# More attention units by rows, a fourth buffer for P, and group loads in the queue of the turns

## The chip, the cores and the metric

The kernel runs on one core of one Trainium2 chip. Its time is the device time of one execution in microseconds (us); medians over several executions are given, with lowest and highest. All runs here are of the state "fast" (on one core there is no second die to compare with). A change counts as faster or slower from 2% on; the effects in this case are far smaller, so ratios are given with a 95% interval.

## The reference

One transformer block for 2048 tokens of width 512, in bfloat16: a grouped-query attention with cached K and V (32 query heads, 8 K/V heads of 128, 2048 keys), then a gated MLP. Both are wrapped in a layer norm whose shift, scale and gate rows come from a condition vector `c`.

```python
mod = (_silu(c) @ w_mod).reshape(c.shape[0], 6, 1, -1)      # sa, ca, ga, sb, cb, gb
h = _layernorm(x, axis=-1) * (1 + ca) + sa
x = x + ga * _A_ref(h, A_k_cache, A_v_cache, A_wq, A_wo)    # attention
h = _layernorm(x, axis=-1) * (1 + cb) + sb
x = x + gb * _B_ref(h, B_w_in, B_w_sp, B_b_sp, B_w_out)     # gated MLP
# in _A_ref:
scores = jnp.einsum('bhqd,bhkd->bhqk', q, k) * Dh ** (-0.5)
p = _softmax(scores, axis=-1)
o = jnp.einsum('bhqk,bhkd->bhqd', p, v)
```

`ga` and `gb` matter below: they are the two rows of the modulation that the kernel spreads over all 128 partitions, by way of the chip's main memory.

## The kernel before

The attention is a loop over **units**. A unit is 128 queries of one K/V group with its four heads; there are 128 of them (16 query tiles for each of 8 groups). A unit has eight **slots**. In each slot TensorE (PE) computes two score matmuls of this unit, ScalarE (ACT) the exponential of them, and PE then does an eighth of the PV product (probabilities times V) of an *earlier* unit and some filler (Q projection or output projection Wo).

There are two kinds of unit:

- **plain**: scores with keys on partitions. PV can use the exponentials as they are, in 64 matmuls of 129 columns, whose extra column of ones gives the softmax sums.
- **by rows**: scores with queries on partitions. ACT writes each head's row into one of six *row buffers* and sums it as it goes, VectorE (DVE) divides the row by its sum, and a transposing DMA, a **turn** of 128 x 2048, issued by SyncE (SP), puts it with keys on partitions into the unit's P buffer. PV is then 16 matmuls of 512 columns, cheaper on PE (8.64 against 8.80 us for the unit in the trace of before), but it needs all four turns to have landed.

```python
TURN_A, TURN_B = 2 * CT, NU - 2                # 8 and 126

def by_rows(u):
    return TURN_A <= u < TURN_B and u % 2 == 0

def pv_at(u):                                  # in which unit the PV of u runs
    return u + 3 if by_rows(u) else u + 1

users, homes = dict(pT0=-2, pT1=-1, wsp=CT + 2), {}   # three P buffers
for u in range(NU):
    homes[u] = min(users, key=lambda k: users[k])
    assert users[homes[u]] < u
    users[homes[u]] = pv_at(u)

def turn_rows(u, hh):                          # two slots after the head's last exponential
    # ... tot = sum of the two halves, rinv = 1 / tot (DVE)
    rows = rows_of(u, hh)
    nc.vector.tensor_scalar(out=rows, in0=rows, scalar1=rinv, scalar2=None, op0=ALU.mult)
    nc.sync.dma_start_transpose(out=pTs[u][:, :, hh * P : (hh + 1) * P], in_=rows)
```

Work that is not of the rhythm itself is put into a calendar, `at(unit, slot, function)`, which sets its place in the program. Four entries matter below. The modulation rows `ga` and `gb` are computed in unit 5, written to main memory as 512 values of 4 bytes each, and read back onto all partitions. The weights of each next group are loaded by GpSimd (POOL), behind a one-element copy that makes POOL wait for a unit's turns (up to 113.4 us in the trace). The first weight matrix of the MLP, `win_sb`, 1792 KB, is loaded in unit 126; three of the six row buffers lie in its place.

```python
def mod_rows():
    # ... mod_part(0), mod_part(1): 32 matmuls of one column
    for i, (part, rows) in enumerate(((2, ga_rows), (5, gb_rows))):
        cols = slice(part * NDT, (part + 1) * NDT)
        nc.vector.tensor_copy(out=modc[:, cols], in_=mc_ps[:, i * NDT : (i + 1) * NDT])
        line = dram.tile([D], FP32, name=f"mod{part}")
        nc.gpsimd.dma_start(out=line[:].rearrange("(dt p) -> p dt", p=P), in_=modc[:, cols])
        nc.gpsimd.dma_start(out=rows[:], in_=line[:].partition_broadcast(P))

at(NU - 2, 4, lambda: nc.gpsimd.dma_start(out=win_sb, in_=win_dram))
at(4, 4, mod_cols_b)
at(5, 4, mod_rows)
# ... for each later group: at(u + 1, 5, after_rows(u)), then at(u + 1, 5, load) on POOL
```

## Time and profile before

| | before |
|---|---|
| median of 3 runs | 1313.34 us (1312.97 to 1314.31) |
| span of the profiled execution | 1311.5 us |
| start to unit 8 | 81.73 us |
| units 8 to 13 | 49.40 us |
| units 14 to 111 | 854.56 us |
| units 112 to 126 | 129.63 us |
| from unit 127 to the end (last PVs, MLP) | 196.16 us |

Below the first two rows, a unit begins with its first exponential on ACT, taken from the trace's records; the last five rows add up to the span. (In the middle this reads 8.87 and 8.57 for the two kinds; the prediction counts from PE's first scores and has 8.64 and 8.80. The pairs are the same.)

PE carries the time almost alone, as the prediction shows with the page's lines. What it does not show is the list of DMA issues, with the median time from issue to landing as the last figure. I had not read these three lines of the kernel before as a warning:

```profile
oT<-onorm SPq DMA_TRANSPOSE x69, 2.8
...
hT<-xn SPq DMA_TRANSPOSE x12, 6.1
...
mod<-modc POOLq DMA_DIRECT2D x2, 2.0 KB, 12.7
```

Only one transfer of the kernel, a load of 1 KB (1.8 us), is smaller than the two writes of the modulation rows, and these took the longest to land. Transposes of the same size, 128 x 512, land in 2.8 us in one place and in 6.1 in another.

### The profile page before, as it was taken

What the parts mean: (1) busy time and instruction counts of PE and PEld (TensorE: products, weight loads), DVE (VectorE), ACT (ScalarE), POOL (GpSimd) and SP (SyncE); (2) the same over time, 40 slices, a digit from 0 to 9 for tenths busy, and PEclk for the clock granted to TensorE, in tenths of its full rate; (3) what the DMA queues carried; (4) which work ended last, traced back from release to release, by engine and by line L of the source; (5) the groups of instructions that cost most, each with busy time, mean ns of one, the idle gap of its engine ahead of it and who ended that gap; (6) DMA issues with size and microseconds to landing.
All of it is one profiled execution on the core that took longest, in us unless ns stands there. A gap on an engine that the chain in (4) does not pass through costs nothing.

```text
span 1311.5 us, 24369 instructions
## 1 busy us (share of the span) xinstructions
PE 1303.8 (99%) x9527; PEld 736.9 (56%) x9527; DVE 689.5 (53%) x1693; ACT 1113.0 (85%) x1533; POOL 59.4 (5%) x115
## 2 busy tenths in 40 slices
PE   9999999999999999999999999999999999999998
PEld 5665555555555555555555555555555555644445
DVE  5644455444454544444445454444445588784444
ACT  7899999999999999999999999999999999550000
POOL 1200000000000000000000000000000011120000
PEclk9999999999999999999999999999999999999999
DMA  6669778877897677867886778668876688364300
GB/s 181 154 97 157 130 128 154 158 118 133 158 166 149 121 144 155 144 125 140 160 169 122 133 157 156 125 127 153 175 143 125 118 140 144 103 133 96 82 21 27
DMA packets 607723, 174.45 MB, mean 133 GB/s; under 512 B 597264, under 2 KB 603664, under 8 KB 607600
## 3 DMA queue, kind: packets, MB, share of 16 engines
q1 hardware_dynamic: 600576, 153.67, 64.9%
q0 software_dynamic: 4432, 16.91, 4.1%
q10 hardware_dynamic: 2592, 2.23, 0.5%
q8 instruction: 77, 1.26, 0.4%
q14 instruction: 46, 0.38, 0.1%
HBM read 21.89 MB, written 2.10 MB: 18 GB/s over the span
## 4 chain that ended last, share of the span: by engine, by line
PE 96%; DVE 2%; DMA 1%; POOL 0%; issue 0%; ACT 0%; DVEq 0%; POOLq 0%
PE o_ps L1080 19%; PE s_ps L1024 18%; PE s_ps L1005 16%; PE o_ps L1059 16%; PE misc L1112 8%; PE misc L945 8%; PE misc L1456 7%; PE s_ps L1290 1%; PE o_ps L1477 1%; DVE stz L1312 1%; PE s_ps L1477 1%; DMA xnT<-xn 0%; DMA wmod_a<-in_w_mod_dram 0%; DVE z L686 0%; POOL rstd_lnz L682 0%; PE misc L855 0%
## 5 line engine op out<-in xcount | busy, mean ns | idle before, releaser
L1031 ACT ACTIVATE pT<-s_ps 128x1024 bf16<-128x1024 f32 x552 | 561.1, 1025 | 30.7 <-PE s_ps L1024 8.7
L1080 PEld LDWEIGHTS <-pT 128*128 128x128 bf16 x4416 | 295.3, 98 | 128.9
L1080 PE MATMUL o_ps<-v,pT 128*128 128x129 bf16 x4416 | 339.7, 220 | 0.0
L1024 PE MATMUL s_ps<-qT,kT 128*128 128x512 bf16 x1104 | 328.1, 379 | 0.3 <-ACT pT L1031 0.2
L1005 PE MATMUL s_ps<-kT,qT 128*128 128x512 bf16 x944 | 280.7, 379 | 0.0
L1012 ACT ACTIVATE win_sb<-s_ps 128x1024 bf16<-128x1024 f32 x238 | 243.7, 1025 | 3.5
L1112 PE MATMUL misc<-wo_g,oT 128*128 128x512 bf16 x512 | 194.0, 379 | 0.0
L945 PE MATMUL misc<-hT,wq_g 128*128 128x512 bf16 (+2 forms) x520 | 187.0, 371 | 0.1
L1024 PEld LDWEIGHTS <-kT 128*128 128x128 bf16 x1104 | 107.3, 98 | 114.9 <-issue 2.3
L1012 ACT ACTIVATE pn<-s_ps 128x1024 bf16<-128x1024 f32 x156 | 159.6, 1024 | 2.0 <-ACT wmod_a L1012 0.3
L1059 PEld LDWEIGHTS <-v 128*128 128x128 bf16 x944 | 92.4, 98 | 111.4
L956 DVE CAST qT<-misc 128x512 bf16<-128x512 f32 x125 | 85.7, 686 | 122.8 <-PE misc L945 122.8
L1068 DVE CAST oT<-o_ps 128x512 bf16<-128x512 f32 x59 | 40.8, 692 | 194.9 <-PE o_ps L1059 194.9
L1059 PE MATMUL o_ps<-wsp,v 128*128 128x512 bf16 x480 | 142.1, 379 | 0.0
L1059 PE MATMUL o_ps<-pT,v 128*128 128x512 bf16 x464 | 138.0, 379 | 0.0
L1005 PEld LDWEIGHTS <-qT 128*128 128x128 bf16 x944 | 92.2, 98 | 61.6
L1045 DVE TENSOR_TENSOR tot<-rs 128x1 f32<-128x1 f32 x236 | 36.4, 154 | 127.1 <-ACT win_sb L1012 84.8
L1456 PE MATMUL misc<-wsp,z 128*128 128x512 bf16 (+2 forms) x560 | 101.4, 336 | 0.2
L1050 DVE TENSOR_SCALAR win_sb<-win_sb,rall 128x2048 bf16<-128x2048 bf16 x119 | 89.7, 753 | 4.4 <-DVE rall L1048 0.3
L1012 ACT ACTIVATE wmod_a<-s_ps 128x1024 bf16<-128x1024 f32 x78 | 79.9, 1025 | 0.0
L1456 PEld LDWEIGHTS <-z 128*128 128x128 bf16 x560 | 50.5, 98 | 49.4 <-DVE z L686 1.6
L1125 DVE TENSOR_TENSOR xacc<-misc,xacc 128x512 f32<-128x512 f32 x112 | 76.2, 680 | 0.0
(110 smaller groups left out, 824.1 us busy)
## 6 DMA issues: line engine op xcount, KB each, us to landing
v<-in_A_v_cache_dram POOLq DMA_DIRECT2D x7, 512.0 KB, 6.6
wq_g<-in_A_wq_dram POOLq DMA_DIRECT2D x7, 512.0 KB, 3.9
wo_g<-in_A_wo_dram POOLq DMA_DIRECT2D x7, 512.0 KB, 4.5
wsp<-in_w_mod_dram POOLq DMA_DIRECT2D x1, 2048.0 KB, 9.1
out_dram<-yout ACTq DMA_DIRECT2D x16, 128.0 KB, 1.7
win_sb<-in_B_w_in_dram POOLq DMA_DIRECT2D x1, 1792.0 KB, 8.0
x_sb<-in_A_x_dram SPq DMA_DIRECT2D x3, 512.0 KB, 6.1
oT<-onorm SPq DMA_TRANSPOSE x69, 2.8
```

The source lines that it names most:

```text
L945: nc.tensor.matmul(ps[0][:, o0 : o0 + n], lhsT=wqs[g][:, dt, hh * DH : (hh + 1) * DH], rhs=hTs[ch][:, dt, c0 : c0 + n], start=(dt == 0), s ...
L956: nc.vector.tensor_copy(out=dst, in_=src)
L1005: nc.tensor.matmul(s_ps[:, c * 512 : (c + 1) * 512], lhsT=qTs[b][:, hh, jj * P : (jj + 1) * P], rhs=groups[g]["kT"][:, k0 : k0 + 512], sta ...
L1012: nc.scalar.activation(out=rows_of(u, hh)[:, half * HK : (half + 1) * HK], in_=s_ps[:], func=ACT.Exp, scale=inv_sqrt_dh, accum_out=rsums[u ...
L1024: nc.tensor.matmul(s_ps[:, h * 512 : (h + 1) * 512].rearrange("p (r q) -> p r q", r=REP), lhsT=groups[g]["kT"][:, kt * P : (kt + 1) * P], ...
L1031: nc.scalar.activation(out=pTs[u][:, 2 * i : 2 * i + 2, :], in_=s_ps[:].rearrange("p (k q) -> p k q", k=2), func=ACT.Exp, scale=inv_sqrt_dh,)
L1050: nc.vector.tensor_scalar(out=rows, in0=rows, scalar1=rinv, scalar2=None, op0=ALU.mult)
L1059: nc.tensor.matmul(o_pss[u][:], lhsT=groups[g]["v1"][:, kt, 0:DH], rhs=pTs[u][:, kt, :], start=(kt == 0), stop=(kt == NKT - 1),)
L1080: nc.tensor.matmul(o_ps[:, hh % 2, 0 : DH + 1], lhsT=pTs[u][:, kt, hh * P : (hh + 1) * P], rhs=groups[g]["v1"][:, kt, 0 : DH + 1], start=( ...
L1112: nc.tensor.matmul(X_ps[:], lhsT=oTs[u][:, hh, :], rhs=groups[g]["wo"][:, hh, :], start=(hh == 0), stop=(hh == REP - 1),)
L1125: nc.vector.tensor_tensor(out=xaccs[j][:], in0=X_ps[:], in1=xaccs[j][:], op=ALU.add)
L1456: nc.tensor.matmul(g_ps[:, :n], lhsT=z2[:, st, f * P : (f + 1) * P], rhs=wsp[t][:, st, c0 : c0 + n], start=(st == 0), stop=(st == NT - 1 a ...
```

## The change

The intent is to cut PE's work further. In units 8 to 111 three of five units go by rows instead of one of two, 69 in all instead of 59. So that turns may come closer together, *every* unit in that stretch has its PV three units later; that needs a fourth P buffer. The 2 MB of `x` are not needed between the first layer norm and the last group, so their place is taken, and `x` is loaded again in the last group. The group loads move from POOL to SP, the queue of the turns, and need no waiting copies there. The modulation moves from units 4 and 5 to unit 9, the first unit without PV work, and the load of `win_sb` a little earlier.

```diff
+    TURN_A, TURN_B = 2 * CT, (HKV - 1) * NT
+    kinds = [
+        TURN_A <= u < TURN_B and (u - TURN_A) % 5 in (0, 2, 3)
+        or TURN_B <= u < NU - CT and u % 2 == 1
+        for u in range(NU)
+    ]
     def pv_at(u):
-        return u + 3 if by_rows(u) else u + 1
+        return u + 3 if TURN_A <= u < TURN_B or by_rows(u) else u + 1
-    users, homes = dict(pT0=-2, pT1=-1, wsp=CT + 2), {}
+    users, homes = dict(pT0=-2, pT1=-1, x=TURN_A + 1, wsp=TURN_A + 2), {}
...
+        at(it, 5, rows)        # mod_b(it): the writes of ga and gb, by POOL
+        for k, (part, dst) in enumerate(((2, ga_rows), (5, gb_rows))):
+            at(it + 4 + k, 5, ... nc.sync.dma_start(...))          # the read-backs, by SP
...
-    at(NU - 2, 4, lambda: nc.gpsimd.dma_start(out=win_sb, in_=win_dram))
-    at(4, 4, mod_cols_b)
-    at(5, 4, mod_rows)
+    at(NU - 3, 6, lambda: nc.gpsimd.dma_start(out=win_sb, in_=win_dram))
+    mod_b(TURN_A + 1)
...
+        it, q = (g - 1) * NT, nc.gpsimd if g == 1 else nc.sync
+        at(*((5, 0) if g == 1 else (it + 5, 5)), lambda g=g, q=q: load_v(g, q))
         # ... load_wq at it + 7, load_wo at it + 9, in the same way
+    for ch in range(NCH):      # x again
+        at(TURN_B + 2 + 2 * ch, 5, ... nc.sync.dma_start(out=x_sb[...], in_=x_dram[...]))
```

(Not printed here: the helper signatures, the fillers' places, when Wo follows.)

More of the change, by code (lines that the diff above doesn't have):

```diff
@@ L723, in load_wq, with load_v @@
         )
-    def load_v(g):
+    def load_v(g, engine):
         v1 = late.tile([P, NKT, DV], BF16, name="v1")
@@ L728, in load_v @@
         if g > 0:
-            nc.gpsimd.dma_start(out=v1[:, :, 0:DH], in_=v_dram[:, g])
+            engine.dma_start(out=v1[:, :, 0:DH], in_=v_dram[:, g])
         else:
@@ L759 @@
     nc.sync.dma_start_transpose(out=kT0[:, HK:SK], in_=A_k_cache[0, 0, HK:SK])
-    load_v(0)
+    load_v(0, nc.sync)
     for ch in range(1, NCH):
@@ L963 @@
     NU = HKV * NT
-    TURN_A, TURN_B = 2 * CT, NU - 2
-    def by_rows(u):
-        return TURN_A <= u < TURN_B and u % 2 == 0
+    TURN_A, TURN_B = 2 * CT, (HKV - 1) * NT
[4 more added lines that the diff above has]
+    ]
+    by_rows = kinds.__getitem__
     def pv_at(u):
-        return u + 3 if by_rows(u) else u + 1
+        return u + 3 if TURN_A <= u < TURN_B or by_rows(u) else u + 1
     def wo_at(u):
-        return pv_at(u) + (3 if u < TURN_B - CT else 2)
-    users, homes = dict(pT0=-2, pT1=-1, wsp=CT + 2), {}
+        return pv_at(u) + (3 if u < NU - 2 * CT else 2)
+    users, homes = dict(pT0=-2, pT1=-1, x=TURN_A + 1, wsp=TURN_A + 2), {}
     for u in range(NU):
-        homes[u] = min(users, key=lambda k: users[k])
+        if u == TURN_B:
+            del users["x"]
+        homes[u] = min(users, key=users.get)
         assert users[homes[u]] < u
@@ L995, in qk @@
                 pTs[u] = wspp.tile([P, NT, 512], BF16, name="wsp")
+            elif homes[u] == "x":
+                pTs[u] = x_sb
             else:
@@ L1038, in rows_of @@
     def rows_of(u, hh):
-        return pn[((u - TURN_A) // 2 * REP + hh) % len(pn)][:, 0:SK]
+        return pn[(sum(kinds[:u]) * REP + hh) % len(pn)][:, 0:SK]
     def turn_rows(u, hh):
@@ L1167, in ln2, with mod_b, begin, cols @@
         at(it + 2, 5, third)
-    def mod_cols_b():
-        mc_ps = bank("misc")
-        for i in range(2):
-            mod_part(i, wmod_b, (1 + i) * D, mc_ps)
-        mod_copy(3, mc_ps)
-    def mod_rows():
-        mc_ps = bank("misc")
-        for i, row in enumerate((0, 3)):
-            mod_part(i, wmod_b, row * D, mc_ps)
-        for i, (part, rows) in enumerate(((2, ga_rows), (5, gb_rows))):
-            cols = slice(part * NDT, (part + 1) * NDT)
-            nc.vector.tensor_copy(out=modc[:, cols], in_=mc_ps[:, i * NDT : (i + 1) * NDT])
-            line = dram.tile([D], FP32, name=f"mod{part}")
-            nc.gpsimd.dma_start(out=line[:].rearrange("(dt p) -> p dt", p=P), in_=modc[:, cols])
-            nc.gpsimd.dma_start(out=rows[:], in_=line[:].partition_broadcast(P))
+    def mod_b(it):
+        ps, lines = {}, {}
+        def begin(k):
+            ps[k] = bank("misc")
+            mod_part(0, wmod_b, (D, 0)[k], ps[k])
+        def cols():
+            mod_part(1, wmod_b, 2 * D, ps[0])
+            mod_copy(3, ps[0])
+        def rows():
+            mod_part(1, wmod_b, 3 * D, ps[1])
+            for i, part in enumerate((2, 5)):
+                c = slice(part * NDT, (part + 1) * NDT)
+                nc.vector.tensor_copy(out=modc[:, c], in_=ps[1][:, i * NDT : (i + 1) * NDT])
+                lines[part] = dram.tile([D], FP32, name=f"mod{part}")
+                nc.gpsimd.dma_start(
+                    out=lines[part][:].rearrange("(dt p) -> p dt", p=P), in_=modc[:, c]
+                )
+        at(it, 1, lambda: begin(0))
+        at(it, 2, cols)
+        at(it, 4, lambda: begin(1))
+        at(it, 5, rows)
+        for k, (part, dst) in enumerate(((2, ga_rows), (5, gb_rows))):
+            at(
+                it + 4 + k,
+                5,
+                lambda part=part, dst=dst: nc.sync.dma_start(
+                    out=dst[:], in_=lines[part][:].partition_broadcast(P)
+                ),
+            )
     def load_wsp(tile_, t, st):
@@ L1229 @@
     at(2, 5, lambda: nc.gpsimd.dma_start(out=wmod_b, in_=wmod_dram[:, :, 2 * D : NMOD]))
-    at(NU - 2, 4, lambda: nc.gpsimd.dma_start(out=win_sb, in_=win_dram))
-    at(4, 4, mod_cols_b)
-    at(5, 4, mod_rows)
+    at(NU - 3, 6, lambda: nc.gpsimd.dma_start(out=win_sb, in_=win_dram))
+    mod_b(TURN_A + 1)
     def set_fill(b):
-        hole = TURN_A + 1 if (TURN_A + 1) // CT == b - 1 else None
+        hole = TURN_A + 2 if (TURN_A + 2) // CT == b - 1 else None
         fs = qproj(b, list(range(REP)), 0, 512, ("misc", "o_ps" if hole else "misc"))
@@ L1241, in set_fill @@
             if hole:
-                it, slot = divmod(hole * NSLOT + k // 2 - 1, NSLOT)
+                it, slot = hole, k // 2
             if b == 1:
@@ L1254 @@
         at(NU + 1 + st // 4, 2 * (st % 4), lambda st=st: load_wsp(wsp[0], 0, st))
-    def after_rows(u):
-        seen = stat.tile([1, 1], BF16, name="seen")
-        nc.gpsimd.tensor_copy(out=seen[:], in_=pTs[u][0:1, NKT - 1, 511:512])
     def after_pv(u):
@@ L1265 @@
     for g in range(1, HKV):
-        it = (g - 1) * NT
+        it, q = (g - 1) * NT, nc.gpsimd if g == 1 else nc.sync
+        at(*((5, 0) if g == 1 else (it + 5, 5)), lambda g=g, q=q: load_v(g, q))
+        at(*((5, 0) if g == 1 else (it + 7, 5)), lambda g=g, q=q: load_wq(g, q))
+        at(*((5, 0) if g == 1 else (it + 9, 5)), lambda g=g, q=q: load_wo(g, q))
         at(it + 11, 5, lambda g=g: load_k(g))
-        loads = (
-            lambda g=g: load_v(g),
-            lambda g=g: load_wq(g, nc.gpsimd),
-            lambda g=g: load_wo(g, nc.gpsimd),
-        )
-        for k, load in enumerate(loads):
-            if g == 1:
-                at(5, 0, load)
-                continue
-            u = next(u for u in range(it + 4 + 2 * k, NU) if by_rows(u))
-            at(u + 1, 5, lambda u=u: after_rows(u))
-            at(u + 1, 5, load)
+    for ch in range(NCH):
+        tiles = slice(ch * CT, (ch + 1) * CT)
+        at(
+            TURN_B + 2 + 2 * ch,
+            5,
+            lambda tiles=tiles: nc.sync.dma_start(
+                out=x_sb[:, tiles, :], in_=x_dram[:, tiles, :]
+            ),
+        )
     zs = {}
@@ L1380 @@
             zs["z2"] = z2p.tile([P, NT, FH], BF16, name="z2")
-        pvs = [u for u in (it - 5, it - 3, it - 1) if 0 <= u < NU and pv_at(u) == it]
+        pvs = [u for u in range(max(it - 3, 0), min(it, NU)) if pv_at(u) == it]
         wos = [u for u in range(max(it - 6, 0), min(it - 2, NU)) if wo_at(u) == it]
```

## The prediction

> **What bounds the kernel now.** I read the page first (busy shares, then the chain that ended last), then the timeline of PE in the middle of the attention and at its start, then the busy table by stretch for the DMA.
>
> ```profile
> PE 1303.8 (99%) x9527; PEld 736.9 (56%) x9527; DVE 689.5 (53%) x1693; ACT 1113.0 (85%) x1533; POOL 59.4 (5%) x115
> ...
> PE 96%; DVE 2%; DMA 1%; POOL 0%; issue 0%; ACT 0%; DVEq 0%; POOLq 0%
> ...
> L1080 PE MATMUL o_ps<-v,pT 128*128 128x129 bf16 x4416 | 339.7, 220 | 0.0
> ...
> L1059 PE MATMUL o_ps<-wsp,v 128*128 128x512 bf16 x480 | 142.1, 379 | 0.0
> L1059 PE MATMUL o_ps<-pT,v 128*128 128x512 bf16 x464 | 138.0, 379 | 0.0
> ```
>
> PE is busy 99% and carries 96% of the chain. The attention is 128 units (16 query tiles for each of 8 groups); in each of its 8 slots PE does two score matmuls for the current unit, one eighth of the PV of an earlier one, and half a filler matmul pair (Q projection, or Wo). PV has two forms: plain, 64 matmuls of 129 columns (4416 / 64 = 69 units), and "by rows", 16 matmuls of 512 columns ((480 + 464) / 16 = 59 units). Busy time cannot price them, since ends are modelled and overlap; starts can:
>
> ```profile
> 505.54 0.59 PE L1024 MATMUL s_ps<-qT,kT 128*128 128x512 bf16 x2
> 505.98 0.59 PE L1059 MATMUL o_ps<-pT,v 128*128 128x512 bf16 x2
> 506.41 0.38 PE L945 MATMUL misc<-hT,wq_g 128*128 128x512 bf16 x1
> 506.62 0.59 PE L1024 MATMUL s_ps<-qT,kT 128*128 128x512 bf16 x2
> ...
> 514.18 0.59 PE L1005 MATMUL s_ps<-kT,qT 128*128 128x512 bf16 x2
> 514.61 0.62 PE L1080 MATMUL o_ps<-v,pT 128*128 128x129 bf16 x8
> 515.06 0.38 PE L945 MATMUL misc<-hT,wq_g 128*128 128x512 bf16 x1
> 515.28 0.59 PE L1005 MATMUL s_ps<-kT,qT 128*128 128x512 bf16 x2
> ```
>
> A slot with PV by rows takes 506.62 - 505.54 = 1.08 us, one with plain PV 515.28 - 514.18 = 1.10 us. The unit from 505.54 lasts 8.64 us, the one from 514.18 to 522.98 lasts 8.80. From unit 14 (first scores at 130.50) to unit 112 (985.06) this alternates unbroken: 98 units, 854.56 us, 8.72 a unit. So plain PV costs about 0.17 us a unit more than PV by rows, and nothing else makes PE wait there. Only where the filler is missing does another engine pace it:
>
> ```profile
> 98.28 0.59 PE L1005 MATMUL s_ps<-kT,qT 128*128 128x512 bf16 x2
> 98.71 0.61 PE L1080 MATMUL o_ps<-v,pT 128*128 128x129 bf16 x8
> 99.29 0.59 PE L1005 MATMUL s_ps<-kT,qT 128*128 128x512 bf16 x2
> ```
>
> That slot holds 0.88 us of PE work and takes 1.01. The timeline of ACT shows its exponentials here at 98.13, 99.12 and 100.12: 1.0 us each with the sum's read-out, its own pace. In a plain unit without backlog from elsewhere they follow at 0.90 (four intervals after 91.35). Call these ACT's floors: 8.0 us for a unit by rows, 7.2 for a plain one, against 8.64 to 8.80 of PE in the middle.
>
> [...]
>
> **The change part by part.**
>
> *More PV by rows.* In units 8 to 111 three of five, 63; in 112 to 123 every odd one, 6; together 69, and 59 plain. Ten units change over: 10 x 48 = 480 matmuls less (the built program has 960 PE rows fewer, 480 weight loads and 480 matmuls). 10 x 0.17 = **-1.7 us**, on the path.
>
> *Work moved on PE.* The 64 one-column matmuls of the modulation (2 x 0.78 us on the chain) leave units 4 and 5 for unit 9. As PV comes three units later for all, units 9 and 10 have no PV (before: only unit 9), and two PVs meet in unit 113 and again in unit 126. None of this changes PE's sum, but units poor in PE work are paced by ACT. I go through them slot by slot, taking the longer of PE's work and ACT's floor, after one slot of grace for the two score buffers. Unit 8 loses two Q matmuls: 8.64 - 0.43 = 8.21. Unit 9 has 5.9 us of PE work under a floor of 7.2: 7.25. Units 10 and 11 (by rows, fillers doubling only the second half): 4 x 1.0 less the grace, plus 4 x 1.08, about 8.12 each. Unit 12 (plain): 4 x 1.10 + 4 x 0.90 = 8.0. Unit 13 (by rows): 8.14. Sum 47.84, against 49.39 before (from 81.10 to 130.50). By columns the PE work in these six is 47.94 before and 45.02 after: the time lost to ACT is 1.45 before and 2.82 after, **+1.4 us**. In unit 4, without the modulation matmuls, ACT's floor costs under 0.1; unit 124 (6.9 us of PE work under 7.2) replaces losses of 0.28 and 0.15 in 124 and 125, and unit 127 adds 0.1: together 0.
>
> *DVE and ACT.* Each unit more by rows adds four times (0.15 + 0.16 + 0.75) us to DVE, less 2 x (0.17 + 0.42) and plus 0.69: about 3.8 us, 38 in all on an engine at 53%. ACT adds about 0.1 us a score tile, 8 us in all. Over five units ACT's floors are 3 x 8.0 + 2 x 7.2 = 38.4 us against PE's 3 x 8.64 + 2 x 8.80 = 43.5. Both lie beside PE.
>
> *DMA.* 40 more turns of 128x2048, 10 fewer of 128x512; x again, 2 MB; the loads in SP's order.
>
> ```profile
> core 0: us, PE busy (x) PEld busy (x) DVE busy (x) ACT busy (x) POOL busy (x), PEclk, DMA share, GB/s
> 550.00:690.00 140.00, 140.00 (x1029) 79.36 (x1027) 68.26 (x169) 136.44 (x193) 3.35 (x7) 1.00 0.76 143
> ...
> 503.00:510.00 7.00, 7.00 (x50) 3.77 (x47) 3.66 (x10) 6.89 (x10) 0.00 (x0) 1.00 1.12 209
> ```
>
> Two units hold 4 big turns and a quarter: 0.76 x 17.44 / 4.25 = 3.1 us of DMA share a turn, loads included. Five units will hold 12.5: 39 us of 43.5, 0.89. While they have work the engines reach 1.12 (packets overlap), so a big turn passes in about 2.8 us at worst. In the two neighbouring units by rows, eight turns come every 2.16 us: the queue grows by at most 0.6 us a turn, 5 us by the eighth. PV, three units on, waits for none of this: the last turn is issued early in the next unit and has about 1.5 units, 13 us, to land. The six row buffers come round tighter. Their shortest reuse falls from 21.8 us to six rows, 13 us, and a row is free about 8 us after its first exponential (497.4 to landing near 505.4). That leaves 5 us[...]. **0 us**, with a risk.
>
> *The rest.* x is back two units before its first use; its buffer's last reader (unit 110's PV) ends before the first reload is issued. The waits on POOL that go were beside everything. The tail after unit 128 keeps its PE work.
>
> Sum: -1.7 + 1.4 = -0.3, rounding aside -0.4: 1313.34 - 0.4 = **1312.9 us**.
>
> **Rivals.** (a) *The row buffers or SP's order become a wait*: ACT waits for a turn, PE for ACT. For: share 0.89, eight turns in a row, head-of-line loads. Against: 5 us of slack. If two neighbouring units by rows lost 0.5 us in each of 21 cycles: +10 us, 1323. (b) *ACT's floor matters in the middle too*, in neighbouring units by rows with PE at 8.64: 8.0 of 8.64 leaves too much room; a small lag (0.1 us a unit) would make +3. (c) *PE gains more*: if the thin start is filled better than I reckon, the full 1.7 comes through and some of the old 1.45 with it: 1310.5.
>
> **Range and chances.** PE's own sum bounds the gain to about 3 us; surprises are mostly waits, so the range leans up: 1310.8 to 1317.0. Faster by over 2% needs 26 us: 0.01. Slower by over 2% needs every cycle to lose 1.2 us: 0.02. Within 2%: 0.97.
>
> **What would show it.** Right: unit starts in the middle at 8.64 and 8.80 with no idle PE; 59 x 64 matmuls of 129 columns; units 8 to 13 in about 47.8 us; unit 113 near 12.3. Wrong: ACT or PE idle on a turn's landing in the third or fourth unit of a cycle, turns landing later than 9 us, DVE waiting on x, or unit times that differ by more than the PV form explains.

## The result, and the profile after

| | before | changed |
|---|---|---|
| median of 4 runs | 1313.61 us (1312.97 to 1314.31) | 1319.78 us (1319.48 to 1324.99) |
| span of the profiled execution | 1311.5 | 1317.5 |
| start to unit 8 | 81.73 | 80.46 |
| units 8 to 13 | 49.40 | 49.94 |
| units 14 to 111 | 854.56 | 852.62 |
| units 112 to 126 | 129.63 | 142.11 |
| from unit 127 to the end | 196.16 | 192.37 |

The ratio is 1.0056 [1.0031, 1.0082]. A ratio is the mean time of one kernel's fast runs over the mean of the other's in the same rounds, so it is not quite the ratio of the medians. By the 2% rule this is "same", but the changed kernel is about 6 us slower and lies outside the range that I had given.

On the page of the changed kernel everything that the change was meant to do is done:

```profile
PE 1295.9 (98%) x8885; PEld 716.6 (54%) x9047; DVE 726.5 (55%) x1783; ACT 1108.7 (84%) x1613; POOL 38.1 (3%) x77
...
L1087 PE MATMUL o_ps<-v,pT 128*128 128x129 bf16 x2496 | 191.1, 220 | 0.4
L1066 PE MATMUL o_ps<-pT,v 128*128 128x512 bf16 x527 | 158.1, 379 | 2.5 <-DVE win_sb L1057 1.8
```

There are 480 weight loads fewer than before (9047 against 9527), as forecast. The plain matmuls are split by P buffer: 2496 here, and 640 each in the `x` and `wsp` buffers, together 3776 = 59 x 64. (Some records of the matmuls by rows are missing, 8885 of 9047 in all, so PE's busy time is not compared.) But the PV line by rows has idle time in front of it where before it had 0.0. The list of all waits (engine and line, what it waited for: us in total, times, longest) has two large entries of PE that the kernel before does not have:

```profile
PE o_ps L1066 <- DMA wsp<-pn: 2.2, 1, 2.2
PE o_ps L1066 <- DVE win_sb L1057: 1.8, 1, 1.8
```

Two waits, once each, both of a PV by rows. They lead to nearly all of the loss, so I look at each.

**The first stall, in unit 11.** The timeline of PE (start, us, line, output and inputs, count, and in brackets the idle time before):

```profile
103.54 0.59 PE L1012 MATMUL s_ps<-kT,qT 128*128 128x512 bf16 x2
105.90 0.60 PE L1066 MATMUL o_ps<-pT,v 128*128 128x512 bf16 x2 [1.76 <-DVE win_sb L1057]
```

The second line is the first PV of unit 8, in unit 11. The profile puts the wait down to DVE, but DVE's last row of unit 8 had been done for 12 us; here the engine named is not the releaser. What had not landed is that row's turn. The issues of both queues around it:

```profile
93.32 2.80 SPq L1058 DMA_TRANSPOSE pT<-wmod_a  x1
...
93.32 1.59 POOL L1194 DMA_DIRECT2D mod<-modc  x2 [34.90 <-DVE modc L1192]
```

And, from the trace's records, when each landed:

```
turn of unit 8, row 3      issued 93.32   landed 105.85   12.53 us   (SP)
write of row ga            issued 93.32   landed 102.77    9.46 us   (POOL)
write of row gb            issued 94.15   landed 105.68   11.53 us   (POOL)
```

The turn's completion came 0.17 us after that of the second write, a transfer of another queue. (In e1, e2 and e3 below, which leave this stall in place, it came 0.20, 0.15 and 0.16 us after it.) The bytes of all three had long been moved: by the trace's records the last packets of both queues ended before 98 us, and from 98 to 100 the DMA engines moved nothing. Before, the turn of the same row took 4.27 us (95.31 to 99.57). Over all turns (the query of their source line gives landing times as smallest, median, largest), before and then after:

```profile
DMA to landing us min/median/max: 4.2/4.4/6.3
```

```profile
DMA to landing us min/median/max: 4.2/4.8/12.5
```

**The second stall, in unit 126.** The timeline of PE there:

```profile
1109.01 0.59 PE L1031 MATMUL s_ps<-qT,kT 128*128 128x512 bf16 x2
1111.79 1.02 PE L1066 MATMUL o_ps<-wsp,v 128*128 128x512 bf16 x4 [2.18 <-DMA wsp<-pn]
1112.65 0.93 PE L1031 MATMUL s_ps<-qT,kT 128*128 128x512 bf16 x2
1113.38 1.91 PE L1066 MATMUL o_ps<-wsp,v 128*128 128x512 bf16 x4
```

The second line is the first PV of unit 123. It waits for that unit's last turn (PE's previous matmul ended modelled at 1109.60; by starts, PE could have gone on at 1109.44, two score matmuls after 1109.01, so 2.35 us are lost). Then the same four matmuls that took 1.02 us take 1.91. The issues:

```profile
1100.61 0.83 POOL L1254 DMA_DIRECT2D win_sb<-in_B_w_in_dram  x1
...
1101.03 5.19 SPq L1058 DMA_TRANSPOSE wsp<-pn  x1
```

The load of `win_sb` landed at 1108.37, the turn at 1111.54, 10.52 us after its issue. The busy table by stretch shows what filled the engines, and what came after (columns as in the prediction; the last three are granted clock, DMA share and GB/s):

```profile
1103.00:1107.00 4.00, 4.00 (x44) 2.73 (x41) 2.30 (x5) 3.73 (x4) 0.00 (x0) 1.00 0.96 384
1113.00:1116.00 3.00, 3.00 (x9) 1.08 (x8) 2.90 (x10) 1.02 (x1) 0.00 (x0) 0.50 0.09 18
```

In the first stretch the engines moved 384 GB/s. By the trace's records of single transfers, in the three microseconds from 1104 POOL's queue had 406, 378 and 413 KB and SP's queue, with the turn in it, 9, 13 and 15 KB. In packets they were far nearer to each other: 58, 54 and 59 of POOL's, of up to 7 KB each, against 35, 53 and 59 of SP's, of up to 256 bytes. In the second stretch, after the pause of 2.18 us, TensorE's clock was granted at half speed (0.50), and some 1.5 us more were lost. Before, the load was issued at 1111.36, when all turns had landed (the last at 1110.50). It could not have come before that landing: the last turn then took its row from one of the three row buffers that lie in the place of `win_sb` (236 rows in turn over six buffers: 235 mod 6 = 1), so the load depended on it, and POOL's wait ahead of the load ended at 1110.53. With 276 rows the last one is in a buffer of its own (275 mod 6 = 5; `wsp<-pn` in the issue above), and the dependence is gone.

**The sum.** The middle, where nothing stalls, is as forecast: units 14 to 111 are 1.94 us faster (forecast 1.7). The stalls are 1.8 + 2.35 + 1.5, some 5.7 us, of the 6 us by which the spans differ.

### The profile page after: what moved, and what is told of

Same layout as the page of the kernel before. It is cut to its first block, busy times and chain, and to the rows that moved or that the text cites. A ratio compares the mean times of both kernels' runs of the same rounds, so it can differ in the third digit from the quotient of the medians.

```text
span 1317.5 us, 23423 instructions
## 1 busy us (share of the span) xinstructions
PE 1295.9 (98%) x8885; PEld 716.6 (54%) x9047; DVE 726.5 (55%) x1783; ACT 1108.7 (84%) x1613; POOL 38.1 (3%) x77
## 4 chain that ended last, share of the span: by engine, by line
PE 96%; ACT 1%; DVE 1%; DMA 1%; issue 1%; DVEq 0%
PE o_ps L1066 18%; PE s_ps L1012 18%; PE o_ps L1087 16%; PE s_ps L1031 16%; PE misc L945 8%; PE misc L1119 8%; PE misc L1476 7%; PE s_ps L1310 2%; PE s_ps L1349 2%; PE o_ps L1497 1%; DMA wsp<-pn 1%; ACT pT L1038 1%; PE o_ps L786 1%; PE s_ps L1497 0%; ACT win_sb L1019 0%
## 5 line engine op out<-in xcount | busy, mean ns | idle before, releaser
L1038 ACT ACTIVATE pT<-s_ps 128x1024 bf16<-128x1024 f32 x312 | 314.5, 1026 | 27.4 <-PE s_ps L1031 13.1
L1012 PE MATMUL s_ps<-kT,qT 128*128 128x512 bf16 x1081 | 323.4, 379 | 2.1
L1019 ACT ACTIVATE win_sb<-s_ps 128x1024 bf16<-128x1024 f32 x276 | 282.3, 1024 | 7.1 <-PE s_ps L1012 3.7
L1031 PE MATMUL s_ps<-qT,kT 128*128 128x512 bf16 x944 | 281.3, 380 | 3.2 <-ACT pT L1038 0.8
L1087 PEld LDWEIGHTS <-pT 128*128 128x128 bf16 x2496 | 166.4, 98 | 71.3
L1087 PE MATMUL o_ps<-v,pT 128*128 128x129 bf16 x2496 | 191.1, 220 | 0.4
L1019 ACT ACTIVATE pn<-s_ps 128x1024 bf16<-128x1024 f32 x184 | 188.2, 1024 | 2.0 <-ACT wmod_a L1019 0.3
L1066 PE MATMUL o_ps<-pT,v 128*128 128x512 bf16 x527 | 158.1, 379 | 2.5 <-DVE win_sb L1057 1.8
L1066 PE MATMUL o_ps<-wsp,v 128*128 128x512 bf16 x291 | 88.0, 383 | 2.5 <-DMA wsp<-pn 2.2
L1038 ACT ACTIVATE wsp<-s_ps 128x1024 bf16<-128x1024 f32 x80 | 81.8, 1023 | 4.7
```

Source lines behind the costliest of these rows:

```text
L1012: nc.tensor.matmul(s_ps[:, c * 512 : (c + 1) * 512], lhsT=qTs[b][:, hh, jj * P : (jj + 1) * P], rhs=groups[g]["kT"][:, k0 : k0 + 512], sta ...
L1019: nc.scalar.activation(out=rows_of(u, hh)[:, half * HK : (half + 1) * HK], in_=s_ps[:], func=ACT.Exp, scale=inv_sqrt_dh, accum_out=rsums[u ...
L1031: nc.tensor.matmul(s_ps[:, h * 512 : (h + 1) * 512].rearrange("p (r q) -> p r q", r=REP), lhsT=groups[g]["kT"][:, kt * P : (kt + 1) * P], ...
L1038: nc.scalar.activation(out=pTs[u][:, 2 * i : 2 * i + 2, :], in_=s_ps[:].rearrange("p (k q) -> p k q", k=2), func=ACT.Exp, scale=inv_sqrt_dh,)
L1066: nc.tensor.matmul(o_pss[u][:], lhsT=groups[g]["v1"][:, kt, 0:DH], rhs=pTs[u][:, kt, :], start=(kt == 0), stop=(kt == NKT - 1),)
L1087: nc.tensor.matmul(o_ps[:, hh % 2, 0 : DH + 1], lhsT=pTs[u][:, kt, hh * P : (hh + 1) * P], rhs=groups[g]["v1"][:, kt, 0 : DH + 1], start=( ...
```

## The experiments

Theory W: the two small writes of the modulation rows hold back the completion of turns issued beside them, whatever the queue. Theory L: the load of `win_sb`, issued ahead of the last turn, holds it back. Rivals: the turns as such are too many for the queue (rival (a) of the prediction), or the writes are harmless and the stall in unit 11 has to do with unit 8 being first to fill its buffer.

### Late writes in the program: e1, e2, e3, e4

e1 puts the writes into the program of unit 12, where no PV is due on the turns of unit 8; e2 puts the load at its later place; e3 does both; e4 does the reverse in the kernel *before*, with the writes in unit 9.

```diff
# e1, e3: the writes leave rows() for
+        at(it + 3, 5, write)          # it = 9; the read-backs two units later
# e2, e3
-    at(NU - 3, 6, ... nc.gpsimd.dma_start(out=win_sb, in_=win_dram))
+    at(NU - 2, 4, ... nc.gpsimd.dma_start(out=win_sb, in_=win_dram))
# e4: kernel before, writes and read-backs leave mod_rows for
+    at(9, 5, mod_write)
```

> Only the two small writes of the modulation rows (512 words of 4 bytes each, POOL's queue) move from unit 9 to unit 12; their read-backs move two units as well. Theory A (the last turn of unit 8 is reported landed only when those writes have landed, 105.85 against 105.68 us in the trace, and PV in unit 11 waits 1.93 us for it): that turn lands in 4 to 5 us instead of 12.5, unit 11 takes about 8.1 us instead of 9.9, and the time falls by 1.8 us from the changed kernel, to about 1318.0. Rival B (the queue of turns is simply longer in this kernel, with more turns and thinner units, whatever POOL writes): the turn still lands late, no gain, 1319.8.

> Only the load of the MLP weights (1792 KB, POOL's queue) moves from behind unit 125's slot 6 to unit 126's slot 4, as in the kernel before. Theory A (the load was issued 0.4 us ahead of the last turn, took the DMA engines for 6 us and held that turn to 10.5 us; PE then idled 2.35 us and ran its next matmuls at half pace for another 1.5): the last turn lands in about 5 us, the wait in unit 126 is gone, that unit takes 11.4 us instead of 15.4, and the time falls by 3.9 us, to about 1315.9. Rival B (backlog of turns): the turn still lands after PV needs it, and less than 1 us is gained.

> Both moves together. Theory A: the two stalls add up, 1319.8 - 1.8 - 3.9 = 1314.1 us, that is, the same as the kernel before within 1 us; nothing of the loss is then left to a fuller DMA queue or to ACT. Rival B: most of the 6 us stays.

> The kernel BEFORE, with nothing changed but that its two small modulation writes (and the read-backs after them) are issued in unit 9 instead of unit 5, so that they meet the last turn of unit 8. Theory A: the fewer turns of this kernel do not help; the turn's landing goes from 4.3 us to 10 us or more, PV in unit 11 (first matmul at 106.1 us) waits 1 to 2 us, and the time rises by that, to 1314.6 to 1315.6. Rival B: with DMA share of 0.65 the turn lands in time, and the time stays at 1313.6.

Measured, beside 1313.54 us of the kernel before (11 runs):

| run | median (lowest to highest), runs | ratio | unit 11 | unit 126 |
|---|---|---|---|---|
| e1 | 1318.44 (1316.59 to 1322.14), 6 | 1.0040 [1.0028, 1.0052] | 9.58 | 14.17 |
| e2 | 1316.82 (1314.57 to 1320.31), 6 | 1.0020 [1.0007, 1.0034] | 15.06 | 11.40 |
| e3 | 1314.81 (1314.07 to 1317.27), 5 | 1.0011 [0.9998, 1.0024] | 9.30 | 11.40 |
| e4 | 1313.20 (1313.01 to 1313.68), 5 | 0.9996 [0.9983, 1.0008] | 7.85 | – |

e1 and e4 are misses, and they teach something: nothing had been moved. POOL has so little to do that it runs far ahead of the other engines and issues the write as soon as its data are there. In e1 the writes were issued at 92.82, as in the changed kernel, and the turn again took 12.08 us; in e4 at 60.94 and 70.77, as in the kernel before. Where a write stood in the program of the idle POOL said little about when it ran: put into unit 12, it was issued in unit 9, at 92.82. (The later place of the load in e2 does hold: the layer norm's statistics stand ahead of it there, which POOL ended at 1119.28, and the load was issued at 1119.67.) So e1 is in effect the changed kernel once more, and its median, 1.3 us lower, shows how far that kernel scatters.

e2 shows that the early load makes the second stall: with the load later, the last turn landed in 4.34 us, unit 126 took 11.40, and PE no longer waits there:

```profile
1113.79 0.59 PE L1031 MATMUL s_ps<-qT,kT 128*128 128x512 bf16 x2
1114.22 1.03 PE L1066 MATMUL o_ps<-wsp,v 128*128 128x512 bf16 x4
```

The stall in unit 11 varies from run to run: in the four traces with the write in its old place (changed kernel, e1, e2, e3) unit 11 took 9.91, 9.58, 15.06 and 9.30 us. The turn follows the second write, which took 11.53, 11.16, 14.16 and 10.92 us; in e2 PE waited 4.38 us for it and then ran at half clock from 106.89 to 113.72. This may be why the changed kernel's times scatter (1319.48 to 1324.99).

### Writes held by a dependence: e5, e6, e7, e8

Here the write really waits: a one-element copy on POOL first reads the last column of the P buffer of unit 11. So POOL waits for unit 11's last turn (67.0 us in e5) before it issues the writes. e5 does that alone; e6 adds the later load; e7 instead leaves the load in its new place and has it issued by SP, so it stands *behind* the last turn in the same queue. e8 is the control in the kernel before: it holds the writes until DVE has finished unit 8's last row, so that they are issued beside its last turn.

```diff
# e5, e6, e7
+        def write():
+            seen = stat.tile([1, 1], BF16, name="seen")
+            nc.gpsimd.tensor_copy(out=seen[:], in_=pTs[TURN_A + 3][0:1, NKT - 1, 511:512])
             # ... the two writes
+        at(it + 3, 5, write)
# e6: the load at (NU - 2, 4);   e7:
-    at(NU - 3, 6, ... nc.gpsimd.dma_start(out=win_sb, in_=win_dram))
+    at(NU - 3, 6, ... nc.sync.dma_start(out=win_sb, in_=win_dram))
# e8: kernel before
+        nc.gpsimd.tensor_copy(out=seen[:], in_=rall[0:1, 9 * REP - 1 : 9 * REP])
         # ... both writes, then both read-backs
```

> The earlier attempt to move the two modulation writes moved them in POOL's program only; POOL had nothing to wait for and issued them at 92.82 us as before. Now a one-element POOL copy, which reads the last column block of unit 11's P, stands ahead of them, so that they are issued after unit 11's last turn has landed, near 121 us. Theory A: the last turn of unit 8 lands in 4 to 5 us, unit 11 takes 8.1 us (9.9, 9.6, 9.3 and 15.1 in the four traces with the write in its old place), and the median falls by about 1.8 us against the changed kernel, to 1318.0, with less scatter. Rival B (the fuller queue of turns): unit 11 stays above 9 us.

> The gated write and the later load of the MLP weights. Theory A: no wait of PE on a turn is left anywhere; unit 11 at 8.1, unit 126 at 11.4 us; median 1313.5 us, the same as the kernel before within 0.7 us, which was the forecast for the whole change. Rival B: at least 1 us of waiting on turns remains, 1314.8 or more as with the two moves before.

> The gated write, and the load of the MLP weights left in its early place of the program but issued by SP, in the queue of the turns, where it stands behind the last turn in order. Same bytes at nearly the same time. Theory A (the load hurt because it came from another queue and overtook the turn): the last turn lands in about 5 us, unit 126 takes 11.4 us, median within 0.5 us of the run with the later load, about 1313.5. Rival C (the bytes themselves are too many at this time, whatever the queue): unit 126 stays near 14 to 15 us and the median near 1318.

> The kernel BEFORE, with its two modulation writes held by a one-element POOL copy until DVE has finished with the last row of unit 8 (about 95 us), then issued one right after the other, as in the changed kernel. Theory A: the last turn of unit 8 lands with the second write, 11 to 12 us after its issue instead of 4.3; PV in unit 11 (106.1 us) waits 0.5 to 1.5 us for it; median 1314.1 to 1315.1. Rival B: with this kernel's fewer turns the landing stays under 6 us and the median at 1313.5.

Measured, beside 1313.55 us of the kernel before (9 runs); five runs each:

| run | median (lowest to highest) | ratio | unit 11 | unit 126 |
|---|---|---|---|---|
| e5 | 1316.80 (1316.35 to 1317.88) | 1.0026 [1.0012, 1.0039] | 8.12 | 15.64 |
| e6 | 1313.71 (1313.41 to 1313.94) | 1.0001 [0.9987, 1.0015] | 8.12 | 11.40 |
| e7 | 1313.34 (1313.12 to 1315.41) | 1.0002 [0.9988, 1.0016] | 8.12 | 11.40 |
| e8 | 1314.71 (1314.06 to 1316.17) | 1.0008 [0.9995, 1.0022] | 9.43 | – |

In e5 the turn landed 4.26 us after its issue, and the same place of PE's timeline has no gap and no wait:

```profile
103.35 0.59 PE L1012 MATMUL s_ps<-kT,qT 128*128 128x512 bf16 x2
103.78 0.59 PE L1066 MATMUL o_ps<-pT,v 128*128 128x512 bf16 x2
```

The writes, issued now at 125.66 and 126.49, held back two turns of unit 13 instead (12.39 and 12.01 us), but no engine was waiting for these. The median is 3.0 us below the changed kernel's, in other rounds, where I had expected 1.8; the profiled spans differ by 1.8.

e6 is the whole change without its two stalls. Its units 8 to 13 take 8.27, 7.31, 8.13, 8.12, 8.03 and 8.28 us, together 48.14 (forecast 47.84); PE waits for no turn. So the remainder of the change is worth nothing measurable: 1.0001. In the profile units 14 to 111 gain 1.93 us, and the other parts together lose 2.1 (forecast 1.4).

e7 was to show by what means L acts, by queue or by bytes, and does not. The load carries the same 1792 KB; behind the turn in SP's program it was issued at 1104.73 and took 7.54 us. But the turn, issued at 1099.68, had landed at 1104.02, in 4.34 us: the two were never in flight together. So e7 shows that a place behind the turn in the same queue keeps the load out of its way; whether the same overlap within one queue would have hurt is not shown.

e8 makes a stall in unit 11 in the kernel before, whose turns are fewer and whose loads are not in SP's queue. The landing times of its turns, and PE in unit 11:

```profile
DMA to landing us min/median/max: 4.2/4.5/14.0
```

```profile
106.57 0.59 PE L1024 MATMUL s_ps<-qT,kT 128*128 128x512 bf16 x2
108.68 0.60 PE L1059 MATMUL o_ps<-wsp,v 128*128 128x512 bf16 x2 [1.52 <-DMA wsp<-wmod_a]
```

Thus rival (a), too many turns, is not needed for unit 11. But e8 does not show that the writes alone do it: its turn landed at 108.64, 4.9 us after the second write (103.78), where I had expected it together with it. POOL had meanwhile issued the read-back of `ga` at 102.26 (landed 108.87), and by the trace's records SP's queue, which moves some 210 KB a microsecond when it is busy (206 from 85 to 87 in the changed kernel), moved only 20 to 39 in each of the five from 97 to 102. What singles out the writes is e9, next. In time e8 is not told apart from the kernel before (its interval includes 1); the trace decides here, not the ratio.

### Writes in pieces of 16 bytes: e9

The changed kernel with the write's order turned round, so that each partition writes four neighbouring values, 128 pieces of 16 bytes instead of 512 of 4. **Its result is wrong on purpose** (relative error 0.035), since the row in memory is permuted.

```diff
-                    out=lines[part][:].rearrange("(dt p) -> p dt", p=P), in_=modc[:, c]
+                    out=lines[part][:].rearrange("(p dt) -> p dt", p=P), in_=modc[:, c]
```

> WRONG RESULT ON PURPOSE. The changed kernel with both stalls in place, but the two modulation writes lay each partition's four words side by side: 128 runs of 16 bytes instead of 512 of 4, same bytes, same time of issue; the rows read back are permuted, so the output is wrong. If the time of these writes goes by their number of pieces, they land in 4 to 5 us instead of 9.5 and 11.5, the last turn of unit 8 with them or before (5 us instead of 12.5), unit 11 takes 8.1 us, and the median is near 1317.5. If the length of the piece does not matter, both land near 11 us, and unit 11 stays above 9 us.

Measured: 1316.63 us (1315.96 to 1318.13, 6 runs), ratio 1.0029 [1.0017, 1.0041] to 1313.01 us of the kernel before (11 runs). The writes were issued in the old place, at 93.28 and 93.91, and landed in 1.95 and 3.72 us; the turn between them landed in 4.49, and unit 11 took 8.12 us. The issues of the writes, and PE in unit 11:

```profile
mod<-modc POOLq DMA_DIRECT2D x2, 2.0 KB, 2.8
```

```profile
103.50 0.59 PE L1012 MATMUL s_ps<-kT,qT 128*128 128x512 bf16 x2
103.94 0.59 PE L1066 MATMUL o_ps<-pT,v 128*128 128x512 bf16 x2
```

What remains above 1.0 is the second stall (unit 126: 13.94). So it is not any write beside a turn that hurts, but one in 512 pieces of 4 bytes. (Whether their number or their length counts, e9 does not tell: it changes both.)

### How many units by rows the rest can bear: e10, e11, e12, e13

With both stalls away, does the forecast's other worry, rival (a), come true when more rows go? e10 has three of four units by rows (e6's places for write and load), e11 four of five, e12 two of three (on e7).

```diff
-        TURN_A <= u < TURN_B and (u - TURN_A) % 5 in (0, 2, 3)
+        TURN_A <= u < TURN_B and (u - TURN_A) % 4 != 1       # e10;  e11: % 5 != 1;  e12: % 3 != 1
# e13, on e12: the writes wait for unit 13, not unit 11
-            nc.gpsimd.tensor_copy(out=seen[:], in_=pTs[TURN_A + 3][0:1, NKT - 1, 511:512])
+            nc.gpsimd.tensor_copy(out=seen[:], in_=pTs[TURN_A + 5][0:1, NKT - 1, 511:512])
-        at(it + 3, 5, write)
+        at(it + 5, 5, write)                                 # read-backs two units later again
```

> Both stalls removed as in the gated run (1313.7), and three of four units by rows in place of three of five: 78 instead of 63 in units 8 to 111. PE alone: 15 x 0.175 = 2.6 us less, perhaps 0.3 lost in the thin units, 1311.4 us. The risk is the one that the forecast named: four units hold 12.25 big turns, 12.25 x 2.9 = 35.5 us of DMA share in 34.7, a share of 1.02 plus loads[...]; three neighbouring units by rows make the queue 4 to 5 us longer, which just uses up the row buffers' slack of 5 us. If that becomes a wait at each group load, some 18 times 0.3 us comes back, 1316.

> As the last, with four of five units by rows (83 or 84). PE alone: 21 x 0.175 = 3.6 us less, 1310.1. DMA share 16.25 x 2.9 / 43.3 = 1.09 plus loads. Four neighbouring units by rows make the queue 6 us longer, more than the row buffers' slack: here rival (a) of the forecast should at last show, ACT waiting for a row buffer and PE for ACT in every cycle. If 0.5 to 1 us is lost a cycle in 21 cycles, 1320 to 1331; if the queue still hides it, 1310.

> The gated write and the load of the MLP weights on SP (1313.3), with two of three units by rows: 69 instead of 63 in units 8 to 111, never more than two neighbours. DMA share over the middle was 0.77 at one of two, 0.93 at three of five, and stopped at 1.12 at three of four and four of five; by the first two it should be 0.93 + 0.067 x 1.6 = 1.04 here, below 1.12. If only the ceiling matters, no wait appears and PE saves 6 x 0.175 = 1.05 us: 1312.3 us, below the kernel before. If 1.04 is already too close (bursts of eight turns and a group load), waits on row buffers appear as at three of four and the time rises above 1314.

> As the last run (two of three by rows, 1319.0), with the two small writes held until the last turn of unit 13 has landed instead of unit 11's; nothing else. In the last run they were issued at 125.4 us, among the first turns of the neighbouring units 13 and 14, whose row buffers are needed again six rows later without a plain unit between: the second turn landed in 13.4 us, ACT waited 4.8 us for its buffer, units 14 and 15 took 13.4 and 10.9 us, and everywhere else the units ran at 8.63 and 8.81. If the writes alone were the cause, units 14 and 15 return to 8.63 to 8.81, the turns that the writes hold back now have a plain unit before their buffers are reused, and the median is 1312 to 1313, 1 us below the kernel before. If bursts of eight turns at a DMA share of 1.03 are the cause, the loss of 6 us stays somewhere.

(The 2.9 us of DMA share a turn, expected in e10 and e11, is the trace's: in the kernel before, from 140 to 980 us, packets of 256 bytes took 22.6 ns each in the mean, and a turn of 512 KB has 2048 of them, for 16 engines: 2.89.)

| run | median (lowest to highest), runs | ratio | before in the same rounds |
|---|---|---|---|
| e10 | 1342.71 (1337.68 to 1344.50), 5 | 1.0219 [1.0202, 1.0237] | 1313.01, 11 runs |
| e11 | 1375.20 (1372.51 to 1379.15), 5 | 1.0472 [1.0454, 1.0490] | 1313.01, 11 runs |
| e12 | 1319.05 (1318.75 to 1320.49), 5 | 1.0038 [1.0025, 1.0052] | 1314.47, 9 runs |
| e13 | 1312.88 (1311.66 to 1323.57), 14 | 1.0010 [0.9994, 1.0026] | 1313.52, 19 runs |

e10 and e11 are far beyond what I had expected (1316; 1320 to 1331). The same stretch of the middle of before, changed kernel, e10, e12 and e13 in the busy table (the column before the last is the DMA share):

```profile
140.00:980.00 840.00, 840.00 (x6159) 476.04 (x6158) 409.04 (x1012) 819.30 (x1156) 20.07 (x42) 1.00 0.77 145
```

```profile
140.00:980.00 840.00, 834.38 (x5620) 457.72 (x5725) 447.31 (x1108) 818.40 (x1241) 1.22 (x6) 1.00 0.93 167
```

```profile
140.00:980.00 840.00, 821.87 (x4912) 418.21 (x4912) 488.74 (x1206) 800.63 (x1320) 1.22 (x6) 0.99 1.12 197
```

```profile
140.00:980.00 840.00, 834.39 (x5303) 444.65 (x5400) 467.69 (x1155) 816.88 (x1286) 1.23 (x6) 1.00 1.03 183
```

```profile
140.00:980.00 840.00, 834.90 (x5336) 445.40 (x5432) 468.32 (x1157) 818.22 (x1286) 1.23 (x6) 1.00 1.05 183
```

(Small differences of PE busy among these mean little, as some matmul records are missing.) The share of 0.77 became 0.93 in the changed kernel, where I had forecast 0.89. At 1.12, the share that the prediction had seen in a short stretch (one of 7 us in the changed kernel, 503 to 510, shows 1.23), the backlog no longer clears between the group loads: in e10 ACT waits for row buffers in units 28, 44, 60, 76, 92 and 108, always the unit after a K load, 10.2 to 13.0 us each (units 14 and 15, at 16.02 and 12.53, are the collision with the writes that e12 shows next). e11, at the same share of 1.12, waits in every cycle. In e10 units 16 to 111 take 853.6 us where 833.1 would be without waits: 20.5 us. The largest entry of ACT's waits on DMA in e10 says it directly:

```profile
ACT wmod_a L1019 <- DMA wsp<-wmod_a: 16.3, 8, 4.0
```

That is rival (a), real, but two steps of density further on than the changed kernel.

e12 looked like a smaller case of it, and is not. All its units 16 to 111 are at 8.63 or 8.81 us; the time is lost in units 14 and 15 (13.42 and 10.90). There ACT waits for a row buffer, and PE's clock then stood at half from 138.96 to 145.79:

```profile
139.34 1.02 ACT L1019 ACTIVATE win_sb<-s_ps 128x1024 bf16<-128x1024 f32 x1 [4.79 <-DMA pT<-win_sb]
```

The writes of the modulation rows, held to 125.43 and 126.26, landed at 136.97 and 137.87, and unit 13's turns beside them took 13.41 and 10.49 us. In e5 the same collision had cost nothing; there unit 14 is plain, while in e12 it goes by rows too and wants a row buffer at once. My tests of W moved the trouble, and in e12 it met somebody.

e13 moves the writes behind unit 13, and the loss is gone: in its profile (span 1310.5) no unit from 14 to 111 is over 8.81 us, at a share of 1.05. The writes, issued at 137.24, still held two turns for 12.72 and 11.15 us, with nobody waiting. Eleven of its 14 runs lie between 1311.66 and 1314.92, but three, which were not profiled, took 1320.38, 1321.10 and 1323.57. The record gives their granted clock: 0.996, 0.997 and 0.995, against 0.999 or more in the other eleven and 0.996 to 0.998 in e12. That points to a pause of PE and half clock there too, but without a profile it is not shown. The better median (by 0.6 us) is therefore no proof of a version that beats both kernels.

## Why the prediction was wrong

By its steps:

- **More PV by rows, -1.7 us**: right. Units 14 to 111 took 852.62 us instead of 854.56, -1.94, all but the first at 8.63 or 8.81, with no wait of PE on a turn.
- **Work moved on PE, +1.4 us**: the mechanism right, the sum somewhat low. Units 8 to 13 without the stall (e6) took 48.14 us, forecast 47.84; unit 113, with its two PVs, took 12.32, forecast 12.3; but all that lies outside units 14 to 111 lost 2.1 us in e6.
- **DVE and ACT beside PE**: right in the middle (no wait there). But DVE's order mattered once: the last row of unit 123 was normalised at 1099.48, about 6 us after its exponentials, as DVE was working through residual and layer norm ahead of it. That delayed the last turn's issue to 1101.03, behind the load of `win_sb`.
- **DMA, "PV, three units on, waits for none of this: the last turn is issued early in the next unit and has about 1.5 units, 13 us, to land … 0 us"**: **this is the step that failed.** It failed in two terms. The room was smaller: 10.65 us for the last turn of unit 8 (93.32 to 103.97; units 9 and 10 are thin), 8.4 us for that of unit 123 (1101.03 to 1109.44). And the time to land was not the turn's own: I reckoned only with the backlog of turns and group loads, at 2.8 us a turn. But two transfers that the change had *moved next to turns* stretched the landing to 12.53 and 10.52 us. I worked out nothing for them: the writes because they are 2 KB, the load of `win_sb` because it had been beside everything before.
- **The rest, "the waits on POOL that go were beside everything"**: true of the copies, but I looked only at what a wait had cost and not at what an order had protected. The load of `win_sb` had been tied to the last turn by its row buffer; I noticed neither that the new count of rows unties it nor that its new slot comes ahead of that turn.
- **Rivals**: (a) named the right effect, a late turn, with the wrong cause and place: row buffers, backlog, every cycle. Its price of 0.5 us a cycle did not show in the changed kernel; in e10 waits of this kind came to 20.5 us. The sign "turns landing later than 9 us" came true. (b) and (c) did not happen.

The sum with the measured terms: -0.4 forecast, + 1.8 (unit 11) + 2.35 (unit 126) + 1.5 (half clock) gives 5.3 us, against 6.2 measured in the medians and 6.0 in the profiled spans. Most of the 0.7 that is left is the forecast of the rest: without stalls e6's profiled span is 0.2 us longer than that of the kernel before, not 0.4 shorter. With both stalls taken away the kernel runs at 1313.71 and 1313.34 us (e6, e7), 0.8 and 0.4 from the forecast, and equal to the kernel before.

What ties the turn to the writes in stall one is not shown; the traces give times alone. The turn's completion came 0.17 us after the completion of a write in another queue, with its bytes moved nearly 8 us before. It repeats in e8 for an oT transpose, issued at 93.12, which landed at 103.95, again 0.17 us after the second write (103.78). And it was to be seen in the trace of before: an hT transpose, issued at 59.84, landed at 70.28, next to the first write's 70.07, and an oT transpose, issued at 72.97, landed 13.13 us later at 86.10, next to the second write's 85.95. No PV hung on these. But the last turn of e8 landed at 108.64, 4.9 us after the second write and 0.23 us before the read-back of `ga`, so not every late turn lands with a write. That the writes themselves take so long because of how they are cut in pieces is shown by e9: 1.95 and 3.72 us, against 9.46 and 11.53 in the changed kernel.

In stall two the packets of the two queues were near each other in number, 54 against 53 and 59 against 59 in the microseconds from 1105 and 1106, and the bytes were not: 378 KB against 13 and 413 KB against 15. But no run changed the packet's size, so that this is what stretched the turn to 10.52 us stays an inference.

Half the clock after the pause of unit 126 did not go by the pause's length. Pauses of 2.18 us (changed kernel) and 2.67 (e5), as the timeline gives them, were followed by half clock, those of 2.62 (e1) and 2.38 (e9) were not: unit 126 took 15.42 and 15.64 us in the former, 14.17 and 13.94 in the latter. The clock records of the traces say more. Over the fifteen traces, every spell of half clock within the attention lasts 3.41, 6.83 or 10.24 us: one, two or three steps of 3.41. (The 1105.92 us of full clock before the one in the changed kernel are 324 steps of 10.24 / 3.) Counted in steps from each trace's own clock changes, PE stood idle (by modelled ends) for 2.14 to 3.41 us of the step just before the clock dropped, ten times in the attention, and for at most 1.93 us in any step there after which it did not drop. The pause of the changed kernel lay whole in one step (2.18), that of e5 nearly so (2.14); a border cut that of e1 into 1.87 and 0.74 and that of e9 into 0.97 and 1.41. So pauses of nearly the same length cost the half clock in two of these four traces and not in the other two, and the step before a drop was not idle from end to end (2.14 of 3.41 in e5).

Still open: what ties a turn's completion to a write in another queue; why the time of the second write, and with it unit 11, varies (10.92 to 14.16 us in four traces); whether the load of `win_sb` hurts by its queue or by its bytes; the three slow runs of e13; and whether e13 or something near it is faster than both.

## What to carry to other kernels

When a change moves a small transfer or an early load, look up in the trace how long it takes to land and which urgent transfers will be in flight beside it, in *any* queue; a deadline of 10 us for a turn of 4 us was not safe here beside a write in 512 pieces (12.53 us) or a large load of another queue (10.52 us). To set when a transfer starts, give it a data dependence (e5: issued at 125.66), or put it behind the urgent one in the same queue (e7: 0.71 us after that had landed); its place in the program of an idle engine did not do it (e1: still at 92.82). And when a wait or a dependence goes because it costs nothing, ask what it was holding back.
